# Attention and two mixtures on one core: GpSimd's attention work moved to VectorE and ScalarE

## The chip, the cores and the metric

One core of a Trainium2 chip runs the whole program. The metric is device time in microseconds, the median of repeated executions. A core has five engines, each with its own in-order queue: TensorE (PE, whose weight loads are PEld), VectorE (DVE), ScalarE (ACT), GpSimd (POOL) and SyncE (SP, which here only issues DMAs). They meet through semaphores.

## The reference

```python
scores = scale * q @ k.T                     # 4 batches x 8 heads, 576 x 576, head_dim 64
scores = where(scores >= max - tau, scores, -1e9)
attn = exp(scores - max); attn /= sum(attn) + 1e-9
x = (attn @ v) as 2304 x 512
h = x @ w_in                                 # 512 -> 1024
solu = h * softmax(h)
x2 = (layernorm(solu) * g_ln) @ w_out        # 1024 -> 512
out = softplus(x2 @ w2_in) @ w2_out          # 512 -> 2048 -> 512
```

The weights of both mixtures arrive as 64-bit floats, handed to the kernel as pairs of 32-bit words. The matrix products of the mixtures are split into a high and a low half of each operand.

## The kernel before

**Attention** goes over 16 pairs of heads. A pair has 2 x 576 query rows: four steps of 2 x 128 rows and a tail of 64 rows of each head, the tile `T`. For each step (`scores`) PE makes the scores into the one score buffer `s` of PSUM, DVE takes the negated maximum (L168), ACT the exponential (L170), and DVE multiplies by the mask and sums (`mask`, L177). PE then transposes the weights through the identity (`xgroup` L190 and L198, `xT` L210), ACT copies the transposes from PSUM (L192, L202, L211), and PE multiplies by v (`av`, L252).

**Division by the sums** comes in `rinv`, once for each half of a pair. DVE adds 1e-9 (L219) and takes the reciprocal (L220). For the full rows the reciprocals of the half are spread by GpSimd over 64 columns (`rb`, L227), transposed on PE (`rgroup`, L234), copied by ACT (L236) and multiplied in at the end (L254, DVE). For the tail rows GpSimd scales `T` itself in the second half, in two operations (L224 for 64 columns, which lays the second head's last columns beside the rest, and L225 for 576 columns). The transposes L198 and L210 read that `T`.

**The weights** are rebuilt by `convert`: ACT takes an absolute value (L76), DVE puts sign, exponent and mantissa together (L77, L78, L80), ACT rounds to the high half (L83), and the low half is the difference of the two (L84, GpSimd). `prep_w1` does it for the first mixture in eight pieces of 128 x 1024 while attention runs; `prep_w2` does it for the second mixture in 16 pieces of 128 x 512 for each of its two matrices, after attention.

**Order.** `slot` writes nine slots a pair, in which the second half of the pair before is finished beside the first half of this one. The first mixture (`m1_units`) can begin only once a batch of four pairs is done, so pairs 0 to 3 have little to lie beside them but the weight pieces. The order in each engine's queue is fixed when the program is built, by a planner that weighs readiness by its own costs; the trace shows it to differ from the text here and there: the spread L227 runs between L224 and L225, and the maximum of the next pair's first scores (L168) behind the reciprocal.

Of the kernel before, what the change touches and what calls it, by code (L numbers as in the profile page):

```python
# [12 lines left out]
ALU = mybir.AluOpType  # L13
# [8 lines left out]
P = 128  # L22
# [6 lines left out]
def f(ap):  # L29
    return ap.bitcast(F32)  # L30
# [3 lines left out]
def tile_attention_solu_softplus(ctx: ExitStack, tc: tile.TileContext, q, k, v, tau, w_in, w_out, g_ln, w2_in, w2_out, out):  # L34
    nc = tc.nc
    PSUM = bass.MemoryType.PSUM
    pe, dve, act, pool, sp = nc.tensor, nc.vector, nc.scalar, nc.gpsimd, nc.sync
# [29 lines left out]
    wo1h = wo1.tile([P, 8, DM], F32R, tag="wo1h", name="wo1h")  # L67
    wo1l = wo1.tile([P, 8, DM], F32R, tag="wo1l", name="wo1l")

    def convert(raw, hi, lo, m_, w_, post=None):  # L70

        lw, hw = raw[:, :, 0], raw[:, :, 1]
        u = w_.bitcast(U32)
        act.activation(out=m_, in_=hw.bitcast(F32), func=AF.Abs, scale=2.0 ** -112)  # L76
        dve.tensor_scalar(out=u, in0=lw, scalar1=29, scalar2=None, op0=ALU.logical_shift_right)  # L77
        dve.scalar_tensor_tensor(out=u, in0=m_.bitcast(U32), scalar=3, in1=u, op0=ALU.logical_shift_left, op1=ALU.bitwise_or)  # L78
        yield
        dve.scalar_tensor_tensor(out=u, in0=hw, scalar=0x80000000, in1=u, op0=ALU.bitwise_and, op1=ALU.bitwise_or)  # L80
        if post is not None:
            post(w_)
        act.copy(out=hi, in_=w_)  # L83
        pool.tensor_tensor(out=lo, in0=w_, in1=f(hi), op=ALU.subtract)  # L84
        yield

    def prep_w1():
        raws = {}

        def load(i):  # L90
            r = raws[i] = m1.tile([P, 1024, 2], U32, tag="lh" if i % 2 else "ll", name=f"raw1_{i}")
            if i < 4:
                sp.dma_start(out=r.rearrange("p n t -> p (n t)"), in_=w_in[i * P:(i + 1) * P, :].bitcast(U32))
            else:
                c = 2 * (i - 4)
                sp.dma_start(out=r.rearrange("p (c n) t -> p c (n t)", c=2),
                             in_=w_out[c * P:(c + 2) * P, :].bitcast(U32).rearrange("(c p) e -> p c e", p=P))
        load(0)
        load(1)
        for i in range(8):  # L100
            q_ = m1.tile([P, 1024], F32, tag="ln", name=f"q1_{i}", bufs=3)
            w_ = m1.tile([P, 1024], F32, tag="u", name=f"w1_{i}", bufs=2)
            if i < 4:
                yield from convert(raws[i], w1h[:, i, :], w1l[:, i, :], q_, w_)
            else:
                c = 2 * (i - 4)
                hi, lo = (w[:, c:c + 2, :].rearrange("p c e -> p (c e)") for w in (wo1h, wo1l))

                def post(w_, c=c):
                    for j in range(2):  # L110
                        wj = w_[:, j * DM:(j + 1) * DM]
                        dve.tensor_scalar_mul(wj, wj, g_sb[:, c + j:c + j + 1])
                yield from convert(raws[i], hi, lo, q_, w_, post)
            if i + 2 < 8:
                load(i + 2)
# [100 lines left out]
    def rinv(p, half):  # L216
        z = st[p]
        cols = slice(0, 4) if half == 0 else slice(4, 9)
        dve.tensor_scalar_add(z["rinv"][:, cols], z["sums"][:, cols], 1e-9)  # L219
        dve.reciprocal(z["rinv"][:, cols], z["rinv"][:, cols])  # L220
        if half:

            T, r = z["T"], z["rinv"][:, 8:9]
            pool.tensor_scalar_mul(T[:, 576:640], T[:, 512:576], r)  # L224
            pool.tensor_scalar_mul(T[:, 0:576], T[:, 0:576], r)  # L225
        z["rb"] = at.tile([P, 4, 64], F32, tag="rb", name=f"rb{p}_{half}")
        pool.tensor_copy(out=z["rb"], in_=z["rinv"][:, 4 * half:4 * half + 4].unsqueeze(2).to_broadcast([P, 4, 64]))  # L227

    def rgroup(p, half):

# [26 lines left out]
    def slot(p, s):  # L257
# [6 lines left out]
        if o >= 0:  # L264
            if s == 0:
                av(o, 0)
            elif s == 1:
                rinv(o, 1); xgroup(o, 1, 0); xgroup(o, 1, 2)
            elif s == 2:
                xgroup(o, 1, 4); xgroup(o, 1, 6)  # L270
            elif s == 3:
                xgroup(o, 1, 8); xT(o); rgroup(o, 1)
            elif s == 4:
                av(o, 1)
        if p < 4 * B:
            if s == 4:
                rinv(p, 0)
            elif s == 5:
                xgroup(p, 0, 8)
            elif s == 6:  # L280
                xgroup(p, 0, 0); xgroup(p, 0, 2)
            elif s == 7:
                xgroup(p, 0, 4); rgroup(p, 0)
            elif s == 8:
                xgroup(p, 0, 6)
            if p + 1 < 4 * B:
                if s == 0:
                    load_pair(p + 1)
                elif s == 6:
                    scale_pair(p + 1)  # L290
# [134 lines left out]
    if True:  # L425
# [46 lines left out]
        def prep_w2(pl, src, hi, lo, nbuf):  # L472
            raws = {}

            def load(c):
                raws[c] = pl.tile([P, 512, 2], U32, tag="raw", name=f"raw2_{c}", bufs=nbuf)
                sp.dma_start(out=raws[c].rearrange("p n t -> p (n t)"), in_=src(c))
            for c in range(nbuf):
                load(c)
            for c in range(NC2):  # L480
                q_ = pl.tile([P, 512], F32, tag="q2", name=f"q2_{c}", bufs=2)
                w_ = pl.tile([P, 512], F32, tag="u2", name=f"u2_{c}", bufs=2)
                for _ in convert(raws[c], hi[c], lo[c], q_, w_):
                    pass
                if c + nbuf < NC2:
                    load(c + nbuf)
                yield

        pw = prep_w2(w2a, lambda c: w2_in[c].bitcast(U32).rearrange("p a b -> p (a b)"), [flat(w) for w in w2h], [flat(w) for w in w2l], 2)
        blocks = [(512 * i, 512) for i in range(4)] + [(2048, 256)]  # L490
        xb = {}
# [31 lines left out]
        wo2h = [w2b.tile([P, DM], F32R, tag=f"wo2h{c}", name=f"wo2h{c}") for c in range(NC2)]  # L523
        wo2l = [w2b.tile([P, DM], F32R, tag=f"wo2l{c}", name=f"wo2l{c}") for c in range(NC2)]
        pw = prep_w2(w2a, lambda c: w2_out[c * P:(c + 1) * P, :].bitcast(U32), wo2h, wo2l, 2)
        gs = {}
        psy = {}
# [49 lines left out]
        for i in range(len(seq) + LA):  # L577
            if i < len(seq):
                bi, c = seq[i]
# [64 lines left out]
```

## Time and profile before

| what | value |
|---|---|
| median of 3 runs | 1029.84 us (1029.72 to 1031.33) |
| profiled execution | 1032.55 us |
| its span, first to last instruction | 1030.8 us |
| PE busy | 941.2 us, 91% |
| DVE busy | 707.1 us, 69% |
| ACT busy | 557.1 us, 54% |
| POOL busy | 144.3 us, 14% |
| mean granted TensorE clock | 0.964 |

Attention fills the first half of the span: the last scaling of `T` starts at 486.6 us. The shares of busy time are averages over stretches with different limits, and the rows below are therefore cut by stretch. A granted clock of 1.00 is 2.4 GHz, and 0.50 is 1.2 GHz.

### The profile page before, as it was taken

The page shows a single profiled execution, that of the slowest core. Times are in us where ns is not written, and L with a number is a line of the kernel's source. Part 1 is how long each engine was busy: PE and PEld are TensorE (multiplying, and loading weights), DVE is VectorE, ACT ScalarE, POOL GpSimd, SP SyncE. Part 2 cuts the span into 40 slices and gives each one's busy share as a digit, 9 for nine tenths or more (in the row PEclk, how much of TensorE's full clock was granted, in tenths as well). Part 3 has the DMA queues.
Part 4 walks back from the last instruction along what each step waited for, and adds up shares of the span by engine and source line. Part 5 has one row for each costly group of instructions (what it writes and reads, how often), then busy time and mean ns, then how long its engine had stood idle before and what let it go on. Part 6 is the DMA issues. An engine that isn't in the chain of part 4 may idle for free.

```text
span 1030.8 us, 14708 instructions
## 1 busy us (share of the span) xinstructions
PE 941.2 (91%) x5584; PEld 738.0 (72%) x5584; DVE 707.1 (69%) x1326; ACT 557.1 (54%) x1013; POOL 144.3 (14%) x135
## 2 busy tenths in 40 slices
PE   3687879899899999999979889899999999999997
PEld 2344556677678777867868787677788788888896
DVE  4775568975776767766598729986665665665565
ACT  4544456665665666656565536554444444444453
POOL 1421112211001111111133234321000000000000
PEclk9778889999999999999999889999999999999999
DMA  6431131112311122110454332311100200000010
GB/s 206 151 110 45 43 90 35 48 54 64 94 46 44 50 73 72 48 35 13 145 168 144 101 111 82 122 42 41 42 1 1 81 1 1 22 21 1 1 42 21
DMA packets 37527, 64.66 MB, mean 63 GB/s; under 512 B 4944, under 2 KB 23376, under 8 KB 36944
## 3 DMA queue, kind: packets, MB, share of 16 engines
q1 hardware_dynamic: 37296, 63.43, 19.6%
q8 instruction: 44, 0.72, 0.3%
q10 hardware_dynamic: 160, 0.30, 0.1%
q14 instruction: 27, 0.22, 0.1%
HBM read 49.55 MB, written 14.16 MB: 62 GB/s over the span
## 4 chain that ended last, share of the span: by engine, by line
PE 63%; DVE 20%; ACT 8%; issue 3%; DMA 3%; POOL 2%; SPq 0%; DVEq 0%; ACTq 0%; POOLq 0%
PE y L568 13%; PE h L536 12%; PE w L252 8%; PE w L321 8%; PE s L162 7%; PE w L370 7%; PE w L190 5%; DVE t L548 2%; DVE nm L168 2%; DVE u L78 2%; DVE w L547 2%; ACT E L170 2%; DVE w L554 1%; DVE w L555 1%; DMA raw<-in_w_in_dram 1%
## 5 line engine op out<-in xcount | busy, mean ns | idle before, releaser
L168 DVE TENSOR_REDUCE nm<-s 128x1 f32<-128x576 f32 x144 | 108.5, 753 | 105.0 <-PE s L162 56.5
L170 ACT ACTIVATE E<-s,nm 128x576 f32<-128x576 f32 x128 | 95.5, 746 | 77.1 <-DVE nm L168 76.8
L568 PE MATMUL y<-wo2h,gh 128*128 128x512 f32 x288 | 113.8, 395 | 8.1 <-ACT gh L556 4.2
L162 PE MATMUL s<-k,q 64*128 64x288 f32 (+1 forms) x640 | 106.8, 447 | 13.9 <-ACT q L136 7.0
L536 PE MATMUL h<-x2h,w2h 128*128 128x512 f32 (+1 forms) x320 | 118.5, 370 | 0.0
L536 PE MATMUL h<-x2l,w2h 128*128 128x512 f32 (+1 forms) x320 | 118.4, 370 | 0.0
L536 PE MATMUL h<-x2h,w2l 128*128 128x512 f32 (+1 forms) x320 | 118.2, 369 | 0.0
L568 PE MATMUL y<-wo2h,gl 128*128 128x512 f32 x288 | 112.8, 393 | 4.7 <-DVE gl L557 4.7
L190 PE MATMUL w<-ident,E 128*128 128x128 f32 x576 | 94.3, 298 | 22.6 <-ACT E L170 12.4
L568 PE MATMUL y<-wo2l,gh 128*128 128x512 f32 x288 | 112.9, 392 | 0.0
L177 DVE SCALAR_TENSOR_TENSOR E<-E,etau 128x576 f32<-128x576 f32 x128 | 105.6, 826 | 5.2 <-ACT E L170 2.1
L190 PEld LDWEIGHTS w<-ident,E 128*128 128x128 f32 x576 | 70.5, 151 | 51.6 <-issue 18.8
L549 ACT ACTIVATE w<-w 128x512 f32<-128x512 f32 (+1 forms) x80 | 47.1, 589 | 98.6 <-DVE t L548 98.4
L252 PE MATMUL w<-eT,v 128*64 128x256 f32 (+1 forms) x704 | 94.0, 401 | 2.6 <-ACT eT L202 2.2
L556 ACT CAST gh<-w 128x512 fp32r<-128x512 f32 (+1 forms) x80 | 46.2, 578 | 88.4 <-DVE w L555 88.1
L162 PEld LDWEIGHTS s<-k,q 64*128 64x128 f32 (+1 forms) x640 | 54.9, 183 | 44.3 <-ACT E L170 11.4
L370 PE MATMUL w<-lh,wo1h 128*128 128x256 f32 x288 | 83.7, 291 | 0.0
L252 PEld LDWEIGHTS w<-eT,v 128*64 128x64 f32 x704 | 54.0, 148 | 41.5 <-issue 14.9
L192 ACT COPY eT<-w 128x512 f32<-128x512 f32 x128 | 72.1, 594 | 21.1 <-PE w L190 20.4
L370 PE MATMUL w<-lh,wo1l 128*128 128x256 f32 x288 | 82.0, 285 | 0.0
L557 DVE TENSOR_TENSOR gl<-w,gh 128x512 fp32r<-128x512 f32 (+1 forms) x80 | 52.4, 655 | 42.9 <-ACT gh L556 42.2
L554 DVE SCALAR_TENSOR_TENSOR w<-h,w 128x512 f32<-128x512 f32 (+1 forms) x80 | 51.0, 637 | 44.8 <-ACT w L549 44.8
(98 smaller groups left out, 1898.6 us busy)
## 6 DMA issues: line engine op xcount, KB each, us to landing
raw<-in_w_in_dram SPq DMA_DIRECT2D x16, 512.0 KB, 3.6
raw<-in_w_out_dram SPq DMA_DIRECT2D x16, 512.0 KB, 3.4
v<-in_v_dram SPq DMA_DIRECT2D x16, 320.0 KB, 3.1
x2s<-x SPq DMA_DIRECT2D x36, 128.0 KB, 1.7
x2r<-x2s SPq DMA_DIRECT2D x9, 512.0 KB, 4.0
out_dram<-yo SPq DMA_DIRECT2D x18, 256.0 KB, 2.1
qr<-in_q_dram SPq DMA_DIRECT2D x30, 144.0 KB, 3.0
raw<-in_w_in_dram SPq DMA_DIRECT2D x4, 1024.0 KB, 5.6
```

Source lines behind the costliest of these rows:

```text
L162: pe.matmul(o, z["q"][r, c:c + m], z["k"][r, kc:kc + 288], start=True, stop=True)
L168: dve.tensor_reduce(out=nm, in_=sv, axis=AX.XY, op=ALU.max, negate=True)
L170: act.activation(out=Ev, in_=sv, func=AF.Exp, bias=nm, scale=1.0)
L177: dve.scalar_tensor_tensor(out=E, in0=E, scalar=etau, in1=E, op0=ALU.is_ge, op1=ALU.mult, accum_out=acc)
L190: pe.transpose(bk[:, 256 * ci + P * j:256 * ci + P * j + P], z["E"][2 * half + j][:, ecol(c):ecol(c) + P], ident)
L192: act.copy(out=eT.rearrange("p c q -> p (c q)"), in_=bk)
L252: pe.matmul(o[64 * h:64 * h + 64, :], w_, e, start=(i == 0), stop=(i == 4))
L321: pe.matmul(ps, x_[:, c, P * t:P * t + P], w_[:, c, 512 * n:512 * n + 512], start=(j == 0), stop=(j == 11))
L370: pe.matmul(o, w_[:, c, P * m:P * m + P], l_[:, c, :], start=(j == 0), stop=(j == 23))
L536: pe.matmul(ps, w_[:, kc, :], x_[:, kc, 0:n], start=(j == 0), stop=(j == 11))
L554: dve.scalar_tensor_tensor(out=w_, in0=ps, scalar=0.0, in1=w_, op0=ALU.max, op1=ALU.add)
L568: pe.matmul(y, g_[:, P * j:P * j + P], w_, start=(c == 0 and i == 0), stop=(c == NC2 - 1 and i == 2))
```

## The change

In `rinv` the two scalings of `T` are issued on DVE instead of GpSimd, and the spread of the reciprocals on ACT. `convert` has a new argument that names the engine of the low half, with DVE as its default: `prep_w1` takes the default, and `prep_w2` passes GpSimd and stays as it was. GpSimd keeps one memset of 64 columns a pair (L238) in attention, and the low halves (L84, second mixture) and L505 after it.

```diff
-    def convert(raw, hi, lo, m_, w_, post=None):
+    def convert(raw, hi, lo, m_, w_, post=None, sub=dve):
...
         act.copy(out=hi, in_=w_)
-        pool.tensor_tensor(out=lo, in0=w_, in1=f(hi), op=ALU.subtract)
+        sub.tensor_tensor(out=lo, in0=w_, in1=f(hi), op=ALU.subtract)
...
             T, r = z["T"], z["rinv"][:, 8:9]
-            pool.tensor_scalar_mul(T[:, 576:640], T[:, 512:576], r)
-            pool.tensor_scalar_mul(T[:, 0:576], T[:, 0:576], r)
+            dve.tensor_scalar_mul(T[:, 576:640], T[:, 512:576], r)
+            dve.tensor_scalar_mul(T[:, 0:576], T[:, 0:576], r)
         z["rb"] = at.tile([P, 4, 64], F32, tag="rb", name=f"rb{p}_{half}")
-        pool.tensor_copy(out=z["rb"], in_=z["rinv"][:, 4 * half:4 * half + 4].unsqueeze(2).to_broadcast([P, 4, 64]))
+        act.copy(out=z["rb"], in_=z["rinv"][:, 4 * half:4 * half + 4].unsqueeze(2).to_broadcast([P, 4, 64]))
...
-                for _ in convert(raws[c], hi[c], lo[c], q_, w_):
+                for _ in convert(raws[c], hi[c], lo[c], q_, w_, sub=pool):
```

## Rows read from the trace of the kernel before

**Rows 1.** Busy us (and count) of each engine by stretch, then granted clock, DMA.
```profile
20.00:48.00 28.00, 18.21 (x86) 10.76 (x85) 24.07 (x34) 16.99 (x25) 10.21 (x8) 0.82 0.51 169
48.00:80.00 32.00, 24.33 (x145) 15.23 (x145) 24.18 (x42) 16.23 (x27) 10.48 (x9) 0.79 0.36 111
...
164.00:200.00 36.00, 30.74 (x204) 21.74 (x203) 34.95 (x69) 24.79 (x47) 7.77 (x7) 0.95 0.13 39
...
320.00:380.00 60.00, 59.88 (x454) 45.75 (x455) 41.40 (x95) 37.87 (x73) 6.06 (x10) 1.00 0.19 56
```
**Rows 2.** Chain that ended last, 0 to 215: start us, us, what.
```profile
47.49 1.71 POOL T L225
...
135.56 1.71 POOL T L225
```
**Rows 3.** Waits, whole span: us in total, times, longest; then 205 to 500.
```profile
PE w L198 <- POOL T L225: 11.8, 5, 2.7
...
PE w L198 <- POOL T L225: 1.0, 1, 1.0
```
**Rows 4.** Timeline around 106: start us, us, instruction [idle before <-releaser].
```profile
106.48 0.19 DVE L220 RECIPROCAL rinv<-rinv 128x5 f32<-128x5 f32 x1
...
106.84 0.45 POOL L224 TENSOR_SCALAR T<-T,rinv 128x64 f32<-128x64 f32 x1 [13.89 <-ACT eT L192]
...
107.60 1.72 POOL L225 TENSOR_SCALAR T<-T,rinv 128x576 f32<-128x576 f32 x1
...
109.37 0.33 PE L198 MATMUL w<-ident,T 128*128 128x128 f32 x1 [2.70 <-POOL T L225]
...
110.66 3.75 PE L252 MATMUL w<-eT,v 128*64 128x256 f32 x24
```
**Rows 5.** Groups by line: busy us, mean ns of one | idle before, releaser.
```profile
L348 DVE TENSOR_SCALAR h<-u,m_nmu,m_t 128x1024 f32<-128x1024 f32 x18 | 15.5, 864 | 0.4
...
L311 DVE TENSOR_TENSOR xl<-xr,xh 128x1024 fp32r<-128x1024 f32 x9 | 11.4, 1265 | 3.2 <-ACT xh L310 3.2
...
L112 DVE TENSOR_SCALAR w<-w,g_sb 128x512 f32<-128x512 f32 x8 | 3.7, 476 | 0.0
...
L236 ACT COPY x<-w 128x256 f32<-128x256 f32 x32 | 12.5, 390 | 0.0
...
L136 ACT ACTIVATE q<-qr 128x576 f32<-128x576 f32 x16 | 10.9, 684 | 17.1 <-PE s L162 13.4 <-DMA qr<-in_q_dram 3.7
```
**Rows 6.** Timelines of POOL and of DVE, where their instructions meet.
```profile
22.23 2.66 POOL L84 TENSOR_TENSOR w1l<-w,w1h 128x1024 fp32r<-128x1024 f32 x1 [20.94 <-ACT w1h L83]
26.20 1.36 POOL L227 COPY rb<-rinv 128x256 f32<-128x256 f32 x1 [1.31 <-DVE rinv L220]
...
192.77 2.37 POOL L84 TENSOR_TENSOR wo1l<-w,wo1h 128x1024 fp32r<-128x1024 f32 x1 [9.47 <-ACT wo1h L83]
...
22.59 2.32 DVE L219 TENSOR_SCALAR rinv<-sums 128x4 f32<-128x4 f32 x1
...
46.14 0.17 DVE L219 TENSOR_SCALAR rinv<-sums 128x5 f32<-128x5 f32 x1
...
174.26 0.22 DVE L345 SCALAR_TENSOR_TENSOR m_t<-m_r,m_t 128x1 f32<-128x1 f32 x1
...
193.03 2.12 DVE L345 SCALAR_TENSOR_TENSOR m_t<-m_r,m_t 128x1 f32<-128x1 f32 x1
```
**Rows 7.** Busy us of PE, granted clock, DMA, in stretches of 2 us.
```profile
100.00:102.00 2.00, 0.86 (x5) 1.00 0.20 66
...
106.00:108.00 2.00, 0.67 (x6) 1.00 0.62 192
108.00:110.00 2.00, 0.63 (x5) 0.96 0.00 0
110.00:112.00 2.00, 2.00 (x11) 0.50 0.00 0
```
**Rows 8.** Timeline later, at full clock: the same multiplication by v.
```profile
426.80 2.38 PE L252 MATMUL w<-eT,v 128*64 128x256 f32 x20
```

## The prediction

> **What bounds the kernel now.** I read the busy time by stretch first, because the average hides four different stages. From 320 to 380 PE is busy for 59.88 of 60 us at a granted clock of 1.00 [rows 1]: there PE is the bound, and an engine beside it can only cost something by starving it. In the first pairs PE is not the bound: 18.21 of 28 us, 24.33 of 32, at clocks of 0.82 and 0.79, with DVE at 24.07 of 28 and 24.18 of 32. From 164 to 200 DVE is busy for 34.95 of 36 us. So the first 200 us are a chain through several engines, DVE nearly full in two stretches of it, and whatever becomes shorter there moves all that follows.
>
> The chain of waits, read next, names GpSimd in it: its scaling of the tail rows, 1.71 us, stands on the chain at 47.49 and again at the ends of the next three pairs, the last at 135.56 [rows 2]; these are four in all, first and last shown. The waits say the same from PE's side: the transpose L198 stood waiting for that scaling five times, 11.8 us in all, 2.7 at the longest, and only 1.0 us of this lies between 205 and 500 [rows 3]. That leaves 10.8 us in four waits of 2.7, all ahead of the stretch that PE fills. The timeline shows one whole: the reciprocal ends at 106.67, GpSimd begins at 106.84, needs two scalings with the spread between them, and PE starts at 109.37 after 2.70 us of nothing [rows 4].
>
> Last I looked at where POOL and DVE run at one time. GpSimd's low half runs from 22.23 to 24.89, and a DVE addition on four columns begun inside it ends at 24.91 after 2.32 us; the next one of its kind takes 0.17 us. At the other end of the list the low half at 192.77 ends at 195.14, and a DVE instruction on one column, 0.22 us elsewhere, takes 2.12 us and ends at 195.15 [rows 6]. There are five such DVE instructions beside eight low halves (at 22.59, 38.56, 67.63, 177.41 and 193.03), 1.9 to 2.15 us too long each; first and last are shown.
>
> **The change part by part.** *Tail rows on DVE.* Removed from the path is the time from the reciprocal's end to L198, 2.70 us. In its place stand two DVE instructions. The one on 576 columns lies between L112 (512 columns, 476 ns) and L348 (1024, 864) [rows 5]: by a straight line 476 + 64 x 0.76 = 525 ns. The one on 64 columns lies between the reciprocal on five, 190 ns [rows 4], and the 476; I take 0.21, near the lower row. That is 0.73 us, and 0.05 more from the producer's end to PE (109.32 to 109.37), so PE would start near 107.45 instead of 109.37: 1.92 us earlier. Four times this is 7.7 us. The bounds: by 476 for the large one and 190 for the small one 2.70 - 0.72 = 1.98 each; by 864 and 476 it is 1.31; and if the next maximum (L168, put behind the reciprocal now) were queued ahead of the scalings, 0.7 less. Four times: 2.4 to 7.9. Behind the scalings on DVE waits that maximum, 0.73 us later than now; but ACT's exponential of it stands behind ACT's copies of the tail's transposes, so the scalings on DVE delay nobody on the path. In the other twelve pairs the 0.73 us lies beside PE's other work, except for the one wait of 1.0 us; I count that as won: 1.0.
>
> *The clock.* After the gap the granted clock is 0.50 from 110 to 112, while 106 to 110 had PE busy for 0.67 + 0.63 of 4 us. A single thin stretch, 100 to 102 with 0.86 us, left it at 1.00 [rows 7]. With the wait cut to 0.8 us the gap looks like the second, not the first. The 24 multiplications by v behind it take 3.75 us [rows 4]; 20 of them at full clock take 2.38, so 24 take 2.86 [rows 8]. If the clock holds, 0.89 us more each, 3.6 for four; if not, nothing.
>
> *Low halves on DVE.* Eight subtractions of 128 x 1024. DVE does the same subtraction of that size in L311, 1265 ns: 8 x 1.265 = 10.1 us added. Taken off DVE are the five stretched instructions, 5 x 2.0 = 10.0 us. By stage: three low halves and two stretched instructions in 20 to 48 (3.8 - 4.3 = -0.5); three and one in 48 to 80 (3.8 - 1.9 = +1.9); two and two in 164 to 200 (2.5 - 4.05 = -1.5, and 0.7 back for a tail scaling there). The sum is +0.6 at the worst reading, in which each microsecond of DVE counts. One thing stands beside it: the spread of the reciprocals took 1.36 us at 26.20, on the path, and the ScalarE one is short, 0.9 less. I take -0.3 for all of this, and as bounds -6 (the new ones all fall into DVE's idle time, and the three stretched additions and shifts on the path, some 2.1 each, are won whole) and +10 (each waits for ACT's rounding in its queue, and the stretched ones were idle time anyway). Queued behind a low half on DVE are the maximum and the mask of the running step; for these wait ACT and PE.
>
> The Trainium skill, "GPSIMD Engine Reference" (4.1 Engine selection), calls GpSimd roughly line-rate for operations with one input, which speaks against moving the tail scaling: by that page 576 columns would take near 0.5 us on either engine (an estimate from its 1.2 GHz) and the first part would win next to nothing. The trace has 1.72 us for it [rows 4], so it does not agree; the measurement decides, and no chance is left to a case of this kind.
>
> *Spread on ScalarE.* 32 copies of 256 columns. ACT's nearest rows are L236, 256 columns from PSUM in 390 ns, and L136, 576 columns in 684 [rows 5]; I take 0.43, which is 13.8 us on an engine busy for 37.87 of 60 us in the full stretch [rows 1]. It is hidden there by PE's own work, so I cost it at nothing; where the cover is gone, each costs 0.43 plus ACT's wait for the reciprocal. Bounds: 0 to 20.
>
> *Sum.* 7.7 + 1.0 + 3.6 + 0.3 = 12.6 us off the profiled execution's 1032.55, so 1020.0; that execution is 2.7 above the median of the runs, and on the median's scale it is 1029.84 - 12.6 = 1017.2. In the stretch that PE fills nothing changes, and behind it the program only starts earlier.
>
> **The rivals.** *The clock still falls after the shorter gap.* For it: seven transposes and ACT's copy still lie between the gap and the multiplications, and no row here shows the clock behind that mixture alone. Against: the thin stretch from 100 to 102, which left it at 1.00 [rows 7]. Without the 3.6: 1020.8.
>
> *The low halves cost DVE their full price.* For it: DVE is the fullest engine in 20 to 48 and 164 to 200, and a subtraction that waits for ACT's rounding holds the maxima behind it. Against: the same engine loses 10 us of stretching. With 10.1 added, none of the 0.3, and the clock not held: 1029.84 - 8.7 + 10.1 = 1031.2, no difference that counts.
>
> *ScalarE starves PE (slower).* In the stretch that PE fills, ACT empties PSUM for PE. If the planner puts the spread ahead of those copies, ACT stands at the head of its queue until DVE's reciprocal, and PE's banks stay full. Price: about 22 spreads lie behind 200 us; 0.43 plus a wait of some 0.5 is 0.9 each, 20 us, so 1017.2 + 20 = 1037. It decides from about 0.6 us lost at each spread on (12.6 / 22). For it: ACT serves the reciprocals late in the pair, in order. Against: ACT is idle for over a third of that stretch.
>
> *The change does not reach the tail.* If the next maximum goes ahead of the scalings at all four, 2.8 less, which is within the cases' own spread.
>
> **How the numbers follow.** Forecast with the clock held 0.44, 1017.2, its own range 1011 to 1022; clock falling 0.28, 1020.8; low halves at full price 0.12, 1031; ScalarE starving PE 0.16, 1037. The range from 1009 to 1030 holds the first two, with a gain of 6 on DVE and the best prices of the tail at its lower end, and half of the third. A measurement of this kernel can tell about 0.2%, 2 us, from no change. Faster: the first two cases and a share of the third, 0.75. The same: most of the third, 0.08. Slower: the last and the rest of the third, 0.17.
>
> **What would show it.** Right: POOL no longer on the chain before 500; waits of L198 under 1 us at four places; a clock near 1.00 in the stretch behind each; no DVE instruction of one to five columns over 2 us; pairs 2 and 3 some 2 to 3 us shorter than their 28; 320 to 380 as full as now. Wrong: PE waiting for ACT's copies behind 200, or DVE subtractions on the chain with the maxima behind them.

## The result and the profile after

The changed kernel takes 1014.67 us (median of four runs, 1011.47 to 1016.54), the kernel before 1030.19 beside it: a ratio of 0.984, 95% interval 0.9815 to 0.9866, or 15.5 us less. The forecast was 1017.2. The profiled execution of the changed kernel took 1011.47 us (span 1009.7), the fastest of its four, so single places of its trace lie somewhat below the median.

The busy time by stretch, for the stages of [rows 1] at their new places (columns: stretch, its length, busy us of PE, PEld, DVE, ACT and POOL with their instructions, granted clock, DMA):

```profile
20.00:45.00 25.00, 16.58 (x84) 10.07 (x82) 24.41 (x40) 17.41 (x27) 0.00 (x0) 0.85 0.58 197
45.00:75.00 30.00, 24.29 (x158) 15.87 (x160) 23.91 (x48) 16.77 (x30) 0.15 (x1) 0.78 0.34 112
...
152.00:188.00 36.00, 31.00 (x215) 21.74 (x213) 34.67 (x78) 26.42 (x51) 0.15 (x1) 1.00 0.12 35
320.00:380.00 60.00, 59.46 (x451) 45.38 (x449) 43.51 (x101) 39.33 (x77) 0.30 (x2) 1.00 0.23 67
```

The first stage is three microseconds shorter with nearly the same work on PE in it (84 matmuls for 86), and DVE is now full there (24.41 of 25 us, 24.07 of 28 before). The stretch that PE fills is as full as before, with 2 us more on DVE and 1.5 more on ACT beside it. The granted clock rose from 0.95 to 1.00 in the stage around 170, and hardly moved in the first two.

The chain of waits at the end of the second pair (start us, us, what), which answers to [rows 2]:

```profile
72.65 0.27 DVE T L224
...
72.94 0.53 DVE T L225
...
73.52 0.34 PE w L198
```

GpSimd stands nowhere on the chain ahead of 500. What PE waited for at that transpose, over the whole span (total, times, longest), answers to [rows 3]:

```profile
PE w L198 <- DVE T L225: 2.0, 3, 0.9
```

It was 11.8 us in five waits of up to 2.7. The timeline at the third pair's end answers to [rows 4]:

```profile
97.42 0.19 DVE L220 RECIPROCAL rinv<-rinv 128x5 f32<-128x5 f32 x1
97.65 0.43 ACT L227 COPY rb<-rinv 128x256 f32<-128x256 f32 x1
97.65 0.25 DVE L224 TENSOR_SCALAR T<-T,rinv 128x64 f32<-128x64 f32 x1
97.94 0.52 DVE L225 TENSOR_SCALAR T<-T,rinv 128x576 f32<-128x576 f32 x1
98.38 0.75 DVE L168 TENSOR_REDUCE nm<-s 128x1 f32<-128x576 f32 x1
...
98.52 0.33 PE L198 MATMUL w<-ident,T 128*128 128x128 f32 x1 [0.90 <-DVE T L225]
...
99.47 2.49 PE L252 MATMUL w<-eT,v 128*64 128x256 f32 x24
```

The order on DVE is the one forecast: scalings first, the next maximum behind. PE waits 0.90 instead of 2.70, and the 24 multiplications by v take 2.49 instead of 3.75. The granted clock, by stretches of 4 us (columns as above), around the first, second and third of these places:

```profile
48.00:52.00 4.00, 2.70 (x13) 1.54 (x12) 4.00 (x6) 1.66 (x3) 0.00 (x0) 0.50 0.44 135
68.00:72.00 4.00, 4.00 (x21) 2.88 (x17) 1.67 (x4) 2.52 (x5) 0.00 (x0) 0.57 0.26 68
96.00:100.00 4.00, 2.90 (x23) 1.82 (x23) 2.63 (x7) 3.14 (x8) 0.00 (x0) 1.00 0.49 140
100.00:104.00 4.00, 3.97 (x47) 2.69 (x44) 2.81 (x6) 1.61 (x3) 0.00 (x0) 1.00 0.00 0
```

From the second place on it stays at 1.00 behind the wait (from 120 to 128, at the fourth, too); behind the first it is at its lower level (0.50, 1.2 GHz), and it still falls in the second pair, ahead of the tail. The first place is another case now: L198 waits for nothing there, and PE stands for ACT's exponential ahead of the scores instead:

```profile
46.54 2.29 PE L162 MATMUL s<-k,q 64*128 64x288 f32 x8 [4.56 <-ACT E L170]
```

Last, the DVE additions on four and five columns (duration min, median, max in ns), to [rows 6]:

```profile
L219 DVE TENSOR_SCALAR rinv<-sums x14: 157/170/183, 21.8 to 208.8; 128x4 f32<-128x4 f32 x7, 128x5 f32<-128x5 f32 x7
```

None is stretched any more; the longest was 2322 ns.

Where the 21 us between the two profiled spans came from is read best between fixed marks: DVE's first instruction on a weight (L77), the mask of each pair's tail (L177 writing T), and the end. Each number is a difference of two starts in the timeline of one profiled execution, in us:

| kernel | first L77 | to the tail of pair 0 | pair 0 to 1 | 1 to 2 | 2 to 3 | 3 to 4 | 4 to 5 | last tail to the end |
|---|---|---|---|---|---|---|---|---|
| before | 16.2 | 29.1 | 32.1 | 28.0 | 27.9 | 28.8 | 34.2 | 546.3 |
| changed | 15.7 | 24.9 | 30.8 | 25.0 | 23.6 | 24.0 | 31.8 | 544.4 |
| tail on DVE alone | 16.6 | 29.2 | 31.0 | 23.7 | 23.7 | 25.1 | 34.2 | 544.8 |
| low halves on DVE alone | 14.9 | 24.6 | 32.9 | 27.9 | 28.0 | 29.1 | 32.3 | 547.1 |
| tail and low halves | 14.9 | 24.8 | 30.5 | 24.9 | 24.7 | 25.9 | 32.4 | 546.3 |
| first three low halves back | 14.9 | 29.3 | 30.7 | 23.6 | 23.6 | 24.9 | 32.4 | 546.0 |
| last five low halves back | 16.2 | 24.9 | 34.4 | 24.6 | 24.7 | 25.3 | 34.2 | 545.3 |
| clock alone | 15.1 | 28.6 | 33.5 | 27.1 | 29.6 | 26.5 | 34.1 | 546.0 |

The ten steps that are left out (pair 5 to the last) come to 287.9 to 289.4 us in all of these kernels. The first number lies ahead of everything that the kernels differ in and still moves by 1.7 us; it is no part of any explanation below.

### The profile page after: what moved, and what is told of

Same layout as the page of the kernel before. It is cut to its first block, busy times and chain, and to the rows that moved or that the text cites. A ratio compares the mean times of both kernels' runs of the same rounds, so it can differ in the third digit from the quotient of the medians.

```text
span 1009.7 us, 14607 instructions
## 1 busy us (share of the span) xinstructions
PE 927.1 (92%) x5584; PEld 728.9 (72%) x5584; DVE 714.0 (71%) x1366; ACT 565.6 (56%) x1045; POOL 76.7 (8%) x63
## 4 chain that ended last, share of the span: by engine, by line
PE 57%; DVE 23%; ACT 12%; issue 4%; DMA 3%; SPq 0%; POOL 0%; DVEq 0%; ACTq 0%
PE y L568 12%; PE h L536 12%; PE w L321 7%; PE s L162 7%; PE w L370 6%; PE w L252 6%; PE w L190 4%; ACT E L170 2%; DVE nm L168 2%; DVE t L548 2%; DVE u L78 2%; DVE w L547 2%; DVE w L554 2%; DVE w L555 2%; DVE u L80 1%
## 5 line engine op out<-in xcount | busy, mean ns | idle before, releaser
L168 DVE TENSOR_REDUCE nm<-s 128x1 f32<-128x576 f32 x144 | 108.4, 753 | 83.7 <-PE s L162 47.5
L162 PE MATMUL s<-k,q 64*128 64x288 f32 (+1 forms) x640 | 107.8, 451 | 18.6 <-ACT E L170 10.6
L190 PE MATMUL w<-ident,E 128*128 128x128 f32 x576 | 90.3, 291 | 20.9 <-ACT E L170 10.4
L177 DVE SCALAR_TENSOR_TENSOR E<-E,etau 128x576 f32<-128x576 f32 x128 | 103.8, 812 | 4.5 <-ACT E L170 1.4
L190 PEld LDWEIGHTS w<-ident,E 128*128 128x128 f32 x576 | 67.8, 147 | 49.5 <-issue 19.8
L252 PE MATMUL w<-eT,v 128*64 128x256 f32 (+1 forms) x704 | 86.4, 376 | 5.4 <-ACT eT L202 4.3
L162 PEld LDWEIGHTS s<-k,q 64*128 64x128 f32 (+1 forms) x640 | 55.4, 185 | 49.2 <-ACT E L170 18.1
L370 PE MATMUL w<-ll,wo1h 128*128 128x256 f32 x288 | 81.7, 284 | 0.0
```

The lines of the kernel that those rows point to most:

```text
L162: pe.matmul(o, z["q"][r, c:c + m], z["k"][r, kc:kc + 288], start=True, stop=True)
L168: dve.tensor_reduce(out=nm, in_=sv, axis=AX.XY, op=ALU.max, negate=True)
L177: dve.scalar_tensor_tensor(out=E, in0=E, scalar=etau, in1=E, op0=ALU.is_ge, op1=ALU.mult, accum_out=acc)
L190: pe.transpose(bk[:, 256 * ci + P * j:256 * ci + P * j + P], z["E"][2 * half + j][:, ecol(c):ecol(c) + P], ident)
L252: pe.matmul(o[64 * h:64 * h + 64, :], w_, e, start=(i == 0), stop=(i == 4))
L370: pe.matmul(o, w_[:, c, P * m:P * m + P], l_[:, c, :], start=(j == 0), stop=(j == 23))
```

## The experiments

All times are medians; each ratio is to the kernel before, run beside it on the same chip. Since a profile is one execution of several that differ by a few microseconds, verdicts on the time are the medians', and the traces only say where.

**The parts one at a time.** The tail rows alone:

```
-            pool.tensor_scalar_mul(T[:, 576:640], T[:, 512:576], r)
-            pool.tensor_scalar_mul(T[:, 0:576], T[:, 0:576], r)
+            dve.tensor_scalar_mul(T[:, 576:640], T[:, 512:576], r)
+            dve.tensor_scalar_mul(T[:, 0:576], T[:, 0:576], r)
```

> Only the two scalings of the tail rows go to DVE; the orders of PE and ACT are those of before. Theory (the tail scaling stood on the path at four places, and the clock fell behind it): 8 to 11 us faster than before, the L198 waits gone down from 11.8 to under 5 us. Rival (the gain of the change came from GpSimd's low halves no longer holding up DVE, and the tail wait is replaced by another): less than 2 us.

Measured: 1021.41 against 1030.99, 0.9902 (0.9872 to 0.9933), 9.6 us less. The orders on PE, ACT and SP are those of before, so nothing but the two scalings' engine explains it. L198 waits 3.7 us in all. Its timeline shows both halves of the theory, the multiplications by v at full clock behind the wait (last row) and, with the low halves left on GpSimd, the stretched DVE instructions still there (the same shift takes 1.21 and 3.36 us):

```profile
25.31 1.21 DVE L78 SCALAR_TENSOR_TENSOR w<-q,w 128x1024 uint32<-128x1024 uint32 x1
...
39.11 3.36 DVE L78 SCALAR_TENSOR_TENSOR w<-q,w 128x1024 uint32<-128x1024 uint32 x1
...
103.62 2.49 PE L252 MATMUL w<-eT,v 128*64 128x256 f32 x24
```

In the table the steps from pair 1 to pair 4 lose 4.3, 4.2 and 3.7 us, that from pair 0 to 1 only 1.1. The clock is not what failed there: from 48 to 52 it was 0.55 in the kernel before and is 1.00 in this one, and the first 22 multiplications by v behind the wait take 2.49 us instead of 4.59. The windows of the two, before first, then rows of DVE and PE in this kernel:

```profile
48.00:52.00 4.00, 2.76 (x13) 2.05 (x15) 2.26 (x3) 2.30 (x6) 3.65 (x2) 0.55 0.13 51
48.00:52.00 4.00, 3.48 (x29) 2.37 (x29) 3.83 (x4) 2.54 (x6) 2.17 (x1) 1.00 0.30 117
...
48.77 2.48 DVE L78 SCALAR_TENSOR_TENSOR w<-q,w 128x1024 uint32<-128x1024 uint32 x1 [0.17 <-ACT q L76]
57.75 2.05 DVE L177 SCALAR_TENSOR_TENSOR E<-E,etau 128x576 f32<-128x576 f32 x1
...
59.96 0.45 PE L190 MATMUL w<-ident,E 128*128 128x128 f32 x1 [3.18 <-DVE E L177]
```

DVE has become the path there, and the two low halves still on GpSimd meet other instructions of it than before: L78 takes 2.48 us instead of 1.22 and a mask 2.05 instead of 0.81, where only one shift had been held up, by 0.65 us (57.86 in the kernel before). PE stands 3.18 us for that mask. So the two parts of the change are not independent at this place. The runs of this kernel spread from 1017.91 at a mean granted clock of 0.980 to 1024.88 at 0.965.

The low halves alone:

```
-    def convert(raw, hi, lo, m_, w_, post=None):
+    def convert(raw, hi, lo, m_, w_, post=None, sub=dve):
...
-        pool.tensor_tensor(out=lo, in0=w_, in1=f(hi), op=ALU.subtract)
+        sub.tensor_tensor(out=lo, in0=w_, in1=f(hi), op=ALU.subtract)
...
-                for _ in convert(raws[c], hi[c], lo[c], q_, w_):
+                for _ in convert(raws[c], hi[c], lo[c], q_, w_, sub=pool):
```

> Only the first mixture's low halves go to DVE. Theory (stretched DVE instructions vanish, and some of them lay on the path of pair 0): 3 to 6 us faster, no DVE instruction on one to five columns over 1 us. Rival (8 x 1.22 us more on DVE pay for what the stretching cost): within 2 us of before.

Measured: 1026.16 against 1030.99, 0.9948 (0.9929 to 0.9966), 4.8 us less, where the prediction had 0.3. In the table the gain stands in two places, some 4.4 us before the tail of pair 0 and 1.9 between pairs 4 and 5. The planner also moved work on PE, ACT and DVE here, so this run alone does not show that the stretching is the cause; the runs with work added to GpSimd, below, keep every order.

The spread alone:

```
-        pool.tensor_copy(out=z["rb"], in_=z["rinv"][:, 4 * half:4 * half + 4].unsqueeze(2).to_broadcast([P, 4, 64]))
+        act.copy(out=z["rb"], in_=z["rinv"][:, 4 * half:4 * half + 4].unsqueeze(2).to_broadcast([P, 4, 64]))
```

> Only the spread of the reciprocals goes to ScalarE. Theory (hidden): 0 to 2 us faster, from the one spread of 1.36 us at 26.20 and from the tail's second scaling no longer standing behind it on GpSimd (0.34 us at four places). Rival (ScalarE waits at the head of its queue for the reciprocal and starves PE): 5 us slower or more.

Measured: 1030.76 against 1030.99, 0.9991 (0.997 to 1.0011): nothing. And the two gainful parts together, the spread left on GpSimd:

> Tail rows and low halves on DVE, the spread still on GpSimd; DVE's order is that of the changed kernel. Theory (the two parts add up, the spread does nothing): 12 to 16 us faster than before, within 2 us of the changed kernel. Rival (GpSimd has to be empty for the gain): under 8 us.

Measured: 1015.39 against 1030.99, 0.9841 (0.981 to 0.9872), 15.6 us less, the whole effect. Within their intervals the parts add up: 9.6 + 4.8 + 0.2 = 14.6.

**Is it GpSimd beside DVE that costs?** Two kernels add work to the changed one without taking any away. Beside each low half on DVE, GpSimd writes something that nobody reads: in the first the same difference of two inputs, in the second a copy by a factor of 1.0 of one input, on 832 columns so that it takes about as long. The line that is added to stands unchanged ahead of the semicolon, and the orders on PE, ACT, DVE and SP are those of the changed kernel in both.

```
+        ...; sub is dve and pool.tensor_tensor(out=at.tile([P, 1024], F32, tag="junk", name=f"junk{next(nj)}"), in0=w_, in1=f(hi), op=ALU.subtract)
```

```
+        ...; sub is dve and pool.tensor_scalar_mul(at.tile([P, 1024], F32, tag="junk", name=f"junk{next(nj)}")[:, 0:832], f(hi)[:, 0:832], 1.0)
```

> The changed kernel, and beside each of the eight low halves on DVE GpSimd makes the same difference once more, with two inputs, into a tile that nobody reads. Theory (GpSimd's operation with two inputs holds up DVE's next instruction that reads two inputs or runs at two ports from SBUF): DVE instructions of 2 us and more are back, and 3 to 6 us of the gain are lost, 1018 to 1021. Rival (GpSimd cost only where somebody waited for its result): within 2 us of the changed kernel, 1013 to 1017.

Measured: 1027.49 against 1029.29, 0.9976 (0.9959 to 0.9993). Of the changed kernel's 15.5 us only 1.8 are left, 13.7 are given back; the direction was forecast, the size (3 to 6) was not. Its timeline, POOL's and DVE's rows together:

```profile
22.29 2.55 POOL L84 TENSOR_TENSOR junk<-w,w1h 128x1024 f32<-128x1024 f32 x1 [20.99 <-ACT w1h L83]
22.55 2.40 DVE L219 TENSOR_SCALAR rinv<-sums 128x4 f32<-128x4 f32 x1
...
39.14 2.38 POOL L84 TENSOR_TENSOR junk<-w,w1h 128x1024 f32<-128x1024 f32 x1 [5.91 <-ACT w1h L83]
39.24 3.35 DVE L84 TENSOR_TENSOR w1l<-w,w1h 128x1024 fp32r<-128x1024 f32 x1
```

Each of the eight catches one DVE instruction, whatever its size, and holds it until GpSimd is done or nearly so. The excess over the usual duration is 2.23, 0.95, 2.13, 2.16, 1.71, 0.97, 2.16 and 1.96 us, 14.3 in all. So a two-input operation there costs DVE 1.8 us on average, and the 14.3 come back in the time nearly one for one (13.7). Where the excess is about 1 us, GpSimd's operation first ran beside DVE instructions that read PSUM, the multiplying-in L254 and a maximum L168; these kept their usual length (0.42 and 0.76 us).

> As the run before it, but GpSimd's extra operation has one input (832 columns times 1.0, about as long, some 2.4 us). In the trace of before DVE's instructions ran at their usual length beside GpSimd's one-input scaling of the tail. Theory (two inputs make the hold-up): within 2 us of the changed kernel, 1013 to 1017, and no DVE instruction stretched beyond 1 us. Rival (any GpSimd operation holds up DVE): as slow as the run with two inputs, 1018 to 1021.

Measured: 1017.39 against 1029.29, 0.9877 (0.9857 to 0.9896), so 3.6 us given back, a little more than forecast. The same view:

```profile
21.20 2.60 POOL L84 TENSOR_SCALAR junk<-w1h 128x832 f32<-128x832 f32 x1 [19.90 <-ACT w1h L83]
21.57 0.84 DVE L219 TENSOR_SCALAR rinv<-sums 128x4 f32<-128x4 f32 x1
22.32 1.21 DVE L84 TENSOR_TENSOR w1l<-w,w1h 128x1024 fp32r<-128x1024 f32 x1
...
35.19 2.31 POOL L84 TENSOR_SCALAR junk<-w1h 128x832 f32<-128x832 f32 x1 [4.51 <-ACT w1h L83]
35.28 1.88 DVE L84 TENSOR_TENSOR w1l<-w,w1h 128x1024 fp32r<-128x1024 f32 x1
```

The same length on GpSimd, but DVE is let through in the midst of it: 0.84 us instead of 2.40 for the addition, 1.88 instead of 3.35 for the subtraction, and a subtraction begun later under the first one takes its usual 1.21. Over the eight the excess is 3.8 us, again close to what the time gave back.

**Where do the low halves gain?** From the run of the low halves alone I took it that the gain lay in pair 0. Two kernels put a part of the eight back on GpSimd:

```
-                yield from convert(raws[i], w1h[:, i, :], w1l[:, i, :], q_, w_)
+                yield from convert(raws[i], w1h[:, i, :], w1l[:, i, :], q_, w_, sub=pool if i < 3 else dve)
```

> The changed kernel with the first three of the eight low halves of the first mixture back on GpSimd. Theory (the 4.8 us that the low halves gave lie in pair 0, where the stretched DVE instructions stand on the path): 4 to 6 us slower than the changed kernel, 1018.5 to 1021. Rival (the gain is spread evenly over the eight): three eighths of 4.8, 1.8 us slower, about 1016.5.

Measured: 1017.91 against 1031.50, 0.9865 (0.9841 to 0.9889): 1.9 us of the 15.5 given back by the medians. With `i > 2` and the four of the output weights on GpSimd instead:

> The changed kernel with the last five of the eight low halves back on GpSimd, the first three on DVE. Theory (gain in pair 0 alone): within 1.5 us of the changed kernel, 1013 to 1016. Rival (spread evenly): five eighths of 4.8, 3 us slower, about 1017.7.

Measured: 1018.71 against 1031.50, 0.9873 (0.9851 to 0.9895): 2.7 given back. Both values are the rival's, not mine. But both intervals overlap with the change's own (0.9815 to 0.9866), and the planner moved PE's and ACT's work in both kernels, so the medians alone tell neither from nothing. The traces, of one execution each, show losses at both ends: back in pair 0, 4.4 us before its tail; the later ones 3.6 between pairs 0 and 1, and 2.4 between pairs 4 and 5. The timeline of the kernel with the five back shows two more victims that the list of [rows 6] does not have, a tail scaling and the shift of a weight:

```profile
42.88 2.09 DVE L224 TENSOR_SCALAR T<-T,rinv 128x64 f32<-128x64 f32 x1
52.51 2.82 DVE L77 TENSOR_SCALAR w<-raw 128x1024 uint32<-128x1024 uint32 x1
```

They take 0.25 and 0.69 us elsewhere. Which instruction is caught, and for how long, depends on the order of the moment. In the kernel before, two of the eight low halves (at 30.55 and 49.16) held up nothing: under the first DVE stood waiting for PE, under the second it waited for ACT and then ran a maximum.

**How much of the tail's gain is the clock?** Matmuls of the identity, whose result nobody reads, were put into PE's queue where it waits for the scalings in the first four pairs. First ten of 128 columns in the kernel before:

```
-        bk = bank()
+        bk = bank(); [pe.matmul(bk[:, 384:512], ident, ident, start=True, stop=True) for _ in range(10 if (half, c0) == (1, 8) and p < 4 else 0)]
```

> The kernel before, with ten extra matmuls of the identity with itself into an unread part of the bank of the tail's transposes, in the first four pairs, in or near the gap of 2.7 us in which PE waits for GpSimd. The wait itself stays. Theory (part of the gain is the clock, which falls behind the gap): granted clock 1.00 behind the gaps, 24 multiplications by v in under 3.1 us instead of 3.75, and 2 to 5 us faster than before, 1025 to 1029. Rival (the clock is not decided by that gap, or the extra matmuls cost what the clock gives): 1030 to 1033.

Measured: 1023.38 against 1029.29, 0.9928 (0.9903 to 0.9953), 5.9 us less with GpSimd's scalings still there. But the planner, which saw PE occupied, also put ACT's exponential of the next pair ahead of the tail's copies, so this does not price the clock alone. A second kernel has fourteen of 16 columns; here only PE's queue is longer and all orders are kept:

```
+                [pe.matmul(bk[:, 384:400], ident, ident[:, 0:16], start=True, stop=True) for _ in range(14 if p < 4 else 0)]
```

> The kernel before, with fourteen matmuls of the identity into unread columns of a bank added to PE's queue ahead of the tail's last transpose in the first four pairs, 16 columns each; the orders on ACT, DVE, GpSimd and SP are those of the kernel before, and PE's own work keeps its order too. Only the clock can change. Theory (a part of the gain of the tail's move is the clock that no longer falls in the wait): the stretch behind the wait shows a granted clock near 1.00, the 24 multiplications by v take under 3.1 us instead of 3.75 at three or four places, and the time falls by 2 to 4 us, to some 1026 to 1028. Rival (the clock follows the length of the gap in the pair's real work, and the larger fall of the run with ten wide matmuls was the changed order on ACT): within 1 us of before, and the 24 multiplications still take 3.75.

Measured: 1032.74 against 1031.50, 1.0012 (0.9996 to 1.0029): nothing gained. In its timeline, the multiplications by v behind the first three waits, and at the second place the fillers (L197) and the next pair's scores (L162) behind them in PE's queue; then the windows behind the second, the third and the fourth wait:

```profile
49.54 2.49 PE L252 MATMUL w<-eT,v 128*64 128x256 f32 x22
...
77.33 2.08 PE L197 MATMUL w<-ident 128*128 128x16 f32 x18
79.33 1.24 PE L162 MATMUL s<-k,q 64*128 64x288 f32 x8
...
82.57 2.49 PE L252 MATMUL w<-eT,v 128*64 128x256 f32 x24
...
110.77 4.16 PE L252 MATMUL w<-eT,v 128*64 128x256 f32 x24
```

```profile
80.00:84.00 4.00, 4.00 (x37) 2.98 (x35) 1.02 (x2) 1.93 (x4) 1.09 (x1) 1.00 0.00 0
108.00:112.00 4.00, 4.00 (x19) 3.21 (x21) 0.24 (x2) 1.97 (x4) 0.21 (x1) 0.50 0.00 0
136.00:140.00 4.00, 4.00 (x37) 3.00 (x35) 1.94 (x3) 1.97 (x5) 1.77 (x2) 1.00 0.09 28
```

Neither theory was right as put, and this kernel does not price the clock alone either. In the kernel before, the scores begin with the tail's mask (77.39, the mask at 77.38); here they stand behind fillers and begin 1.7 to 2.2 us after it at all four places (79.33, the mask at 77.18). Behind the second and the fourth wait, where the clock was 1.00, the step to the next tail was all the same 27.1 and 26.5 us against 28.0 and 28.8 before, 0.9 and 2.3 less, where 0.89 was forecast for one place. Behind the first the clock was back at its upper level as well (1.00 from 52 to 56, 22 multiplications in 2.49 us), and yet pair 0 to 1 took 33.5 against 32.1: as in the run of the tail rows alone, the low halves caught L78 (2.65 us) and a mask (2.05), and PE stood 3.19 us for that mask. Behind the third it fell, and the step was 29.6 against 27.9. So a clock of 1.00 can shorten a place; what it is worth in sum, without the fillers' own cost, no run shows, and why the third place fell with the same fillers is open.

Fillers of 128 columns in the changed kernel, four ahead of the tail's transposes in the first four pairs and six ahead of the first half's in three of them:

```
-        bk = bank()
+        bk = bank(); [pe.matmul(bk[:, 384:512], ident, ident, start=True, stop=True) for _ in range({(1, 8): 4, (0, 8): 6 if p else 0}.get((half, c0), 0) if p < 4 else 0)]
```

> The changed kernel with four such matmuls ahead of the tail's transposes and six ahead of the first half's in pairs 1 to 3 (four and none in pair 0). Theory (what the changed kernel's runs differ in is the clock between 45 and 130 us): faster than the changed kernel by 1 to 5 us, 1010 to 1014, with the runs closer together. Rival (the extra matmuls stand on the path, or the planner's order moves): 1015 to 1019.

Measured: 1010.84 against 1029.29, 0.9811 (0.9791 to 0.9832), 18.5 us less than before and 2.9 less than the change. That is the size expected, but the interval overlaps with the change's (0.9815 to 0.9866), and here too the order moved, so it is neither a sure gain nor a price.

**Does the rule carry to the second mixture?** Its 32 low halves of 512 columns stayed on GpSimd in the change.

```
-                for _ in convert(raws[c], hi[c], lo[c], q_, w_, sub=pool):
+                for _ in convert(raws[c], hi[c], lo[c], q_, w_):
```

> The changed kernel with the low halves of the second mixture's weights on DVE too: 32 subtractions of 128 x 512, which the same operation in L362 does in 681 ns, 21.8 us added to DVE between 490 and 700, where it is busy for 32 to 40 of 40 us. Theory (the price is what GpSimd's operation takes from DVE, against the subtraction on DVE itself): the stretched DVE operations there are only some hundreds of ns too long each, so less comes back than is added: between 1 us faster and 7 slower than the changed kernel, likeliest 3 slower, 1017 to 1018. Rival (keeping two-input operations off GpSimd always pays): 3 us faster or more, under 1012.

Measured: 1001.11 against 1031.50, 0.97 (0.9676 to 0.9724). That is 30.4 us less than before, twice the change's gain, and the best kernel of the study; my likeliest value was wrong even in its sign. DVE's groups by line from 480 to 800, first the changed kernel, then this one (busy us, mean ns of one | idle before, releaser):

```profile
L78 DVE SCALAR_TENSOR_TENSOR u<-q,u 128x512 uint32<-128x512 uint32 x32 | 28.5, 890 | 2.3 <-ACT q L76 1.5
...
L77 DVE TENSOR_SCALAR u<-raw 128x512 uint32<-128x512 uint32 x32 | 18.8, 587 | 19.9 <-POOL wo2l L84 15.3 <-DMA raw<-in_w_in_dram 4.5
```

```profile
L78 DVE SCALAR_TENSOR_TENSOR u<-q,u 128x512 uint32<-128x512 uint32 x32 | 22.0, 686 | 0.4
...
L77 DVE TENSOR_SCALAR u<-raw 128x512 uint32<-128x512 uint32 x32 | 13.5, 421 | 5.8 <-DMA raw<-in_w_in_dram 5.5
L84 DVE TENSOR_TENSOR wo2l<-u,wo2h 128x512 fp32r<-128x512 f32 x16 | 11.0, 687 | 14.9 <-ACT wo2h L83 14.6
L84 DVE TENSOR_TENSOR w2l<-u,w2h 128x512 fp32r<-128x512 f32 x16 | 11.0, 685 | 0.1
```

A mean of 890 ns looked like the price of the operation; without GpSimd beside it, it is 686, and the shift L77 falls from 587 to 421. The idle time that moved is not the gain: DVE stood 15.3 us for GpSimd's low halves ahead of L77, and stands 14.6 for ACT's rounding ahead of L84 instead. The windows of the two kernels, changed first:

```profile
600.00:640.00 40.00, 36.28 (x154) 28.07 (x153) 39.69 (x59) 24.00 (x42) 14.90 (x8) 1.00 0.32 105
```

```profile
600.00:640.00 40.00, 40.00 (x179) 33.10 (x178) 38.88 (x71) 26.98 (x47) 0.00 (x0) 1.00 0.28 92
```

From 600 to 640 DVE does 71 instructions in 38.88 us where it did 59 in 39.69, and PE, which waited for it, fills the stretch. DVE's busy time over the whole run is 706.6 us against 714.0, although 22.0 us of subtractions were added: 29.4 came back. The time from the last tail to the end is 529.9 us against 544.4, 14.5 less, which is the gain over the change (30.4 - 15.5 = 14.9). Nine two-input differences (L505) stay on GpSimd even here, and still catch DVE: five additions of L547 take 2.2 us each, where the median of that line is 0.43. Moving these too was not tried, nor the fillers together with all low halves on DVE.

## Why the prediction came out

The total was forecast 2.5 us too high, inside its range, with the chain and the order of the steps as written. Two of its terms were off, in opposite directions, so that the total came this close is in part luck.

**Tail rows and clock: 12.3 forecast, 9.6 measured alone.** The step is confirmed: the two scalings take 0.25 and 0.52 us (0.21 and 0.525 were read from neighbours), the wait is 0.90 at the third place, where 0.8 was forecast, and three of the four places gain. The first gains little alone (1.1 us in the table), although the clock behind it was 1.00: DVE is the path there, and the low halves left on GpSimd took back what PE had won. That place carried a quarter of the term. With the low halves on DVE in both kernels the tail rows take off 10.8 us (1026.16 to 1015.39). At the other three a pair gains more than the 1.92 + 0.89 that were counted, 3.7 to 4.3 us in the profiled run: some 1.8 are the wait, 1.26 the 24 multiplications (they were put at 2.86 us, scaled from a row of 20, and take 2.49), 0.3 the transposes between (1.29 us from L198 to the first multiplication in the kernel before, 0.96 in this run), and the rest no run separates. That the clock is a real part is seen in these multiplications; its share of the 9.6 stays open.

**Low halves: 0.3 forecast, 4.8 measured alone, and this is the step that failed.** The prediction wrote "three low halves and two stretched instructions in 20 to 48 (3.8 - 4.3 = -0.5)", and counted DVE's own time. DVE's windows in the two profiles, from the first L77 to the tail of pair 0, first before, then changed:

```profile
16.23:45.28 29.05, 17.48 (x80) 10.30 (x78) 25.78 (x36) 16.25 (x24) 8.92 (x5) 0.82 0.48 154
```

```profile
15.66:40.53 24.87, 16.24 (x80) 9.92 (x78) 24.17 (x37) 16.71 (x26) 0.00 (x0) 0.87 0.50 171
```

DVE is busy 1.6 us less (0.7 of this a shift that slid behind the mark), so the count of its work was about right. But it was idle for 3.27 us before and is idle for 0.70 now. Nearly all of that was one wait, which the list of waits of before gives as

```profile
DVE x L254 <- PE w L252: 2.3, 1, 2.3
```

and which is not there after. It is the far end of the first stretched addition of [rows 6]: that holds up the reciprocal, this the spread, this PE's transposes of it and the multiplications by v, and DVE stands at the head of its queue for their result. The stretched instruction was paid for twice, once on DVE and once as DVE's own wait for what it had made late. On that chain the spread counts too: it took 1.36 us at 26.20, where the median of the 32 is 0.40, and DVE's two-input L80 had begun just ahead of it, at 26.08. So the prediction's 0.9 for the spread looks like GpSimd held up by DVE, and not like a faster copy on ScalarE (0.40 in the median as well). With the spread on ScalarE and the first three low halves back, the addition (2.41 us) is back and so is a good half of the wait,

```profile
DVE x L254 <- PE w L252: 1.2, 1, 1.2
```

a mask behind it takes 1.68 us instead of 0.81, and the 4.4 us are back as well. The value that came true lies near the prediction's bound of -6, the one in which the new subtractions fall into idle time and the stretched ones are won whole; I had taken a value near DVE's sum, at the other end.

A second reading was too narrow: I counted the five instructions that were some 2 us too long, since there the stretch is plain. A sixth, the shift at 57.86, was 0.65 us too long. In a group of 32 a stretch hides in the mean; that is why the second mixture, where no row looked odd, held another 14.9 us.

**Spread on ScalarE: 0 forecast, 0.2 measured.** The copy takes 0.43 us at the third pair's end, as read from L236 and L136. ACT's queue did not starve PE in the stretch that PE fills: 59.46 of 60 us from 320 to 380.

**The rivals.** The clock still falling has one place in the changed kernel, the first, and behind another wait than the scaling's. Low halves at their full price did not happen: DVE's busy time fell by 1.9 us with them on DVE alone (707.1 to 705.2), 9.8 us of subtractions included. The slower rival, ScalarE starving PE, is excluded by the spread's own run. The signs named in advance held, but for the clock behind the first wait; pairs 2 and 3 are 3.0 and 4.3 us shorter, a little more than the 2 to 3 named.

## What to carry to other kernels

Before an operation is left on GpSimd because it is "off the path", look at what DVE does in the same microseconds: one long instruction among its kind, or a mean above that of the same shape elsewhere, is the price, and it is to be followed to who waits for that instruction's result. Price a move by running the operation alone on the other engine, and try all of its kind once one pays: here eight moved and 32 were left behind, and the 32 were worth nearly as much as the whole change. Expect the parts to touch: a place won on one engine moves the others' instructions under the operation that is left. A shorter wait on PE may bring back the clock behind it, but that part differs from place to place and from run to run, so keep it as a term of its own.

## What the runs showed of the hardware

A two-input GpSimd operation of 2.4 us holds one DVE instruction for nearly all of it, whatever that instruction's size (0.17 us became 2.40, 1.21 became 3.35), while a one-input operation of the same length lets DVE through (0.84 and 1.88). The maxima, which read PSUM, are not held: 0.76 us at 75.21, inside the two-input operation from 74.71 to 77.05 of the first of these kernels. The Trainium skill, "SBUF — State Buffer" (SBUF: two separate sides), calls the ports that the two engines share an exclusive lock, held for the whole instruction by whoever starts first, GpSimd or a VectorE instruction with two inputs in SBUF or in a two-port mode. The two-input rows agree with that; the addition that ended at 22.41 under a one-input operation running until 23.80 does not.

Executions of one program differ by up to 10 us: 23 runs of the kernel before went from 1026.35 at a mean granted clock of 0.968 to 1036.54 at 0.959, and six of the kernel with the tail rows alone from 1017.91 at 0.980 to 1024.88 at 0.965. That is two thirds of what the whole change gained. A difference of two profiles says little until each one's place among its kernel's runs is known.
